# The first Fourier transform of an attention + Fourier mixer kernel: tokens s and 576-s folded before the matmuls

## Chip, cores and metric

One core of a Trainium2 chip. The metric is the time of one execution in microseconds of the device, the median of several runs. Everything is float32 at the interface.

## What is computed

The reference is three layers in a row. The change is in the second, and in the store of the first.

```python
def _moe_ref(x, w_ch1, w_ch2):               # x: (4, 576, 512), the output of the attention
    X = np.fft.fft(x, axis=1)                # over the 576 tokens: "the first transform"
    X = np.fft.fft(X, axis=2)                # over the 512 channels
    mixed = np.real(X).astype(np.float32)
    u = x + mixed
    un = (u - mean(u)) / sqrt(var(u) + 1e-06)
    ch = np.maximum(un @ w_ch1, 0.0) @ w_ch2
    return u + ch
```

Ahead of it stands an attention with 4 batches of 8 heads, 576 tokens and head size 64, and a learned bias; behind it a second mixer (`_moe2_ref`) with a matmul over the tokens.

## The kernel before

The stages follow each other: bias tables, attention, Fourier stage, channel MLP, gated MLP. Float32 products are made of rounded halves ("hi" and "lo", type fp32r), three matmuls for one product.

**Attention.** It walks over 72 pairs of units, one per iteration `d`; `n = d - 72` counts the last ones, and `after(n)` is called at the end of each iteration. Heads are done two at a time, 16 pairs of them (0 to 15), four for each batch. `finish` scales the output of a pair on DVE (L530 to L556), `store` writes it to the DRAM array `xd[b]` (L568, L571) one iteration later. The last pair (15) is not stored: `finish` writes it straight into the Fourier stage's input tile of batch 3 (L556). The last probabilities are transposed on PE (L484), copied by ACT (L486), their low half taken by DVE (L493), and multiplied on PE (L510).

**Loads for the Fourier stage.** `first_folds` calls `Folds.load(0)` at `n` = -3, and `load(1)`, `load(2)`, `load(3)` at `n` = 0, 3 and 4 (`X_LOAD`); each is two transfers on SP's queue (L742, L743), with the 576 tokens on partitions in five blocks `t` of 128. The sine table is loaded at `n` = 0 by POOL (L733), the cosine table during the bias stage (L696).

**Folds.** For real input the second transform needs only sums and differences of channels. `Folds.prep(b)` makes them on DVE in six steps: twice a sum or difference of the upper and lower half (L769, 5 x 256 elements, one operand read backwards), four times a second fold (L757, 635 elements, and L758, 5 elements), ACT rounds it (L759), DVE takes the low part (L763, L764). From `n` = 1 on, two steps for batch 0 are put into each iteration of the attention's end; the other batches' steps stand one by one between the matmul groups of the Fourier stage.

**Fourier stage.** For each batch five groups of the first transform (`p1`, `pe`, `po`, `me`, `mo`; `stage1`, L837), each a sum over the 576 tokens against 290 table columns: four blocks of 128 tokens with three matmuls each, and the last 64 tokens with two, so 14 matmuls. ACT evacuates (L840). `second` is the second transform (L884), `residual` transposes the input on PE (L872), and two DVE additions (L888, L895) write `u`. In batches 2 and 3, weight unpacking (L994 to L1009) and the norm of the first token chunks (L1156 to L1211, with matmuls at L1163) are put into the same places, and then the MLP begins (L1301, L1337).

The order on each engine is set when the program is built, by a list scheduler: an instruction that it takes to be ready can be put ahead of one written earlier. Each engine and each queue then runs in order.

Of the kernel before, what the change touches and what calls it, by code (L numbers as in the profile page):

```python
# [20 lines left out]
DM = 512  # L21
# [323 lines left out]
def attention_phase(tc, nc, io, vs, bias, biasl, raw, xd, ident, last, after, es, right):  # L345
# [172 lines left out]
    def finish(d):  # L518
        c = d % 9
        if c not in (3, 4, 8):  # L520
            return
        ns = (2 * (d // 9), 2 * (d // 9) + 1)
        ns = ns if c == 4 else ns[c // 8 : c // 8 + 1]
        for n in ns:
            if n not in xs:
                xs[n] = xp.tile([128, 5, 128], F32, tag="x", name="x") if n + 1 < len(pairs) else last
        po = outs.pop((d // 9, int(c == 4), int(c == 8)))
        w = 1 if c == 4 else 4
        ri = wp.tile([128, 2, 4], F32, tag="ri", name="ri", bufs=4)[:, :, 0:w]
        nc.vector.tensor_scalar(  # L530
            out=ri, in0=po[:, :, 0:w, 64], scalar1=PSC * 1e-9, scalar2=vs[:, 0:1], op0=ALU.add, op1=ALU.mult
        )
        yield
        nc.vector.reciprocal(out=ri, in_=ri)
        yield
        if c != 4:
            n = ns[0]
            x = xs[n][:, 0:4].rearrange("p t (h d) -> p h t d", h=2)
            nc.vector.tensor_tensor(
                out=x if ahead(n) else x[:, ::-1],  # L540
                in0=po[:, :, :, 0:64],
                in1=ri.rearrange("p h (w o) -> p h w o", o=1).to_broadcast([128, 2, 4, 64]),
                op=ALU.mult,
            )
            return
        for j, n in enumerate(ns):
            x = xs[n]
            if n + 1 < len(pairs):
                nc.vector.tensor_scalar(
                    out=x[:, 4, 0:64], in0=po[:, j, 0, 0:64], scalar1=ri[:, j], scalar2=None, op0=ALU.mult  # L550
                )
                continue
            for a in range(2):
                f = 64 * a if ahead(n) else 64 - 64 * a
                r = slice(64 * a, 64 * a + 64)
                nc.vector.tensor_scalar(  # L556
                    out=x[0:64, 4, f : f + 64], in0=po[r, j, 0, 0:64], scalar1=ri[r, j], scalar2=None, op0=ALU.mult
                )

    def store(d):  # L560
        n = 2 * (d // 9) + (d % 9 == 8)
        if d % 9 not in (4, 8) or n + 1 == len(pairs):
            return
        b, p = pairs[n]
        p = p if ahead(n) else H // 4 - 1 - p
        f = slice(128 * p, 128 * p + 128)
        x = xs.pop(n)
        nc.sync.dma_start(out=xd[b][0:512, f].rearrange("(t p) d -> p t d", p=128), in_=x[:, 0:4])  # L568
        for a in range(2):
            f = 128 * p + (64 * a if ahead(n) else 64 - 64 * a)  # L570
            nc.sync.dma_start(out=xd[b][512:S, f : f + 64], in_=x[64 * a : 64 * a + 64, 4, 0:64])  # L571
# [71 lines left out]
def phases(tc, nc, io, vs, low, raw, xd, ident, tables, last, after, right):  # L643
# [4 lines left out]
    with ExitStack() as es:  # L648
        att = attention_phase(tc, nc, io, vs, bias, biasl, raw, xd, ident, last, after, es, right)
# [26 lines left out]
X_LOAD = 0, 3, 4  # L676
# [5 lines left out]
AFTER = (0,)  # L682


def tables(tc, nc, io, es):
# [4 lines left out]
    tt = cp.tile([128, 10, TP], F32R, name="tt")  # L690

    fs = cp.tile([128, 8, 128], F32, name="fs")
    ident = cp.tile([128, 128], F32, name="ident")

    def load():
        nc.gpsimd.dma_start(out=tt, in_=io["c_t"][:, 0])  # L696
# [4 lines left out]
        nc.sync.dma_start(out=ident, in_=io["c_ident"])  # L701
        yield

    return (tt, fs, ident), load()


class Folds:

    SIZE = 5 * (DM + 1)
    STEPS = 6

    def __init__(self, tc, nc, io, xd, xs, work, temps, es):
        self.tc, self.nc, self.io, self.xd, self.es = tc, nc, io, xd, es
        self.xs = [x.rearrange("p (t f) -> p t f", t=5) for x in xs]
        self.pm = [w.rearrange("p (t f) -> p t f", t=5) for w in work]
        self.temps = [t.rearrange("p (t f) -> p t f", t=5) for t in temps]  # L720
        self.hi, self.lo = [], []
        self.done = -1
        self.flow = self.steps()

    def last(self):

        return self.xs[B - 1][:, :, DM - 127 : DM + 1]

    def open(self):

        p = self.es.enter_context(pool(self.tc, name="ff", bufs=1, side="right"))
        self.sin = p.tile([128, 10, TP], F32R, name="sin")
        self.nc.gpsimd.dma_start(out=self.sin, in_=self.io["c_t"][:, 1])  # L733
        for x in range(2):
            self.hi.append(p.tile([128, 5, DM], F32R, name=f"fhi{x}"))
            self.lo.append(p.tile([128, 4, DM], F32R, name=f"flo{x}"))

    def load(self, b):
        nc, x, d = self.nc, self.xs[b], self.xd[b]
        n = DM if b + 1 < B else DM - 128  # L740
        f = slice(1, n + 1)
        nc.sync.dma_start(out=x[:, 0:4, f], in_=d[0:512, 0:n].rearrange("(k p) d -> p k d", p=128))  # L742
        nc.sync.dma_start(out=x[0:64, 4, f], in_=d[512:S, 0:n])  # L743

    def prep(self, b):
        nc, x, pm = self.nc, self.xs[b], self.pm
        hi, lo = self.hi[b % 2], self.lo[b % 2]
        up, dn = slice(1, 128), slice(255, 128, -1)


        ops = (ALU.add, ALU.subtract, ALU.subtract, ALU.add)
        r = slice(0, 64)

        def high(g):
            s, F = pm[g // 2], self.temps[g % 2]
            c = 128 * (g % 2)
            nc.vector.tensor_tensor(out=F[:, :, 1:128], in0=s[:, :, up], in1=s[:, :, dn], op=ops[g])  # L757
            nc.vector.tensor_copy(out=F[:, :, 0:1], in_=s[:, :, c : c + 1])  # L758
            nc.scalar.activation(out=hi[:, :, 128 * g : 128 * g + 128], in_=F, func=AF.Copy)  # L759

        def low(g):
            F, q = self.temps[g % 2], slice(128 * g, 128 * g + 128)
            nc.vector.tensor_tensor(out=lo[:, :, q], in0=F[:, 0:4], in1=hi[:, 0:4, q].bitcast(F32), op=ALU.subtract)  # L763
            nc.vector.tensor_tensor(  # L764
                out=hi[64:128, 4, q], in0=F[r, 4], in1=hi[r, 4, q].bitcast(F32), op=ALU.subtract
            )

        for z in range(2):
            nc.vector.tensor_tensor(  # L769
                out=pm[z], in0=x[:, :, 256:0:-1], in1=x[:, :, 257 : DM + 1], op=ALU.subtract if z else ALU.add  # L770
            )
            high(2 * z)
            yield
            high(2 * z + 1)
            low(2 * z)
            yield
            low(2 * z + 1)
            yield
# [33 lines left out]
def fft_phase(tc, nc, folds, tabs, ut, bank, extra, es):  # L812
# [7 lines left out]
    tt, fs, ident = tabs  # L820
    xs, need = folds.xs, folds.need
    COS, SIN = tt, folds.sin
# [5 lines left out]
    def stage1(b, nm, col, ncol, t):  # L828
        hi, lo = folds.hi[b % 2], folds.lo[b % 2]
# [12 lines left out]
    def first(b, nm):  # L842
# [3 lines left out]
        need(folds.STEPS * b + dict(p1=2, pe=2, po=2, me=4, mo=5)[nm])  # L846
        stage1(b, nm, *dict(p1=(128, 1, COS), pe=(0, 128, COS), po=(128, 128, SIN), me=(256, 128, COS), mo=(384, 128, SIN))[nm])
# [5 lines left out]
    def gather(b, e):  # L853

        n = 2 * b + e
        if 3 <= n < 2 * B:
            o = 1280 * (n % 2)
            t = parts[n] = room[:, o : o + 1280].rearrange("p (t s c) -> p t s c", t=5, s=2)
# [4 lines left out]
    def residual(b, e, y):  # L863
# [738 lines left out]
def build(tc, io, out):  # L1602
    nc = tc.nc
    with ExitStack() as ctx:
# [14 lines left out]
            [more[:, o : o + 1280], more[:, o + 1280 : o + 2560]],  # L1619
            [raw[:, n : n + 640], more[:, o + 2560 : o + 3200]],  # L1620
            right,
        )
        with ExitStack() as e1:
            e1.enter_context(tc.manual_schedule())
            phases(tc, nc, io, vs, (low, more), raw, xd, tabs[2], load, folds.last(), first_folds(folds), right)
# [76 lines left out]
def consts2():  # L1702
# [7 lines left out]
    tt = np.zeros((128, 2, 10, TP), np.float32)  # L1710
    for n, fn in enumerate((np.cos, np.sin)):
        a = fn(2 * np.pi * ((np.arange(576)[:, None] * t) % 576) / 576)
        h, l = two(a)
        for k in range(4):
            tt[:, n, k] = h[128 * k : 128 * k + 128]
            tt[:, n, 4 + k] = l[128 * k : 128 * k + 128]
        tt[0:64, n, 8] = tt[64:128, n, 8] = h[512:]
        tt[0:64, n, 9] = l[512:]
    c["c_t"] = tt
    d = np.arange(128)[:, None]  # L1720
# [54 lines left out]
```

## Time and profile before

| | us |
|---|---|
| median of 3 runs | 1116.43 (1114.87 to 1120.73) |
| the profiled execution, its own time | 1117.11 |
| its span in the profile | 1115.3 |
| PE busy | 1035.9 (93%) |
| DVE busy | 700.1 (63%) |
| ACT busy | 554.0 (50%) |
| POOL busy | 289.8 (26%) |

The profile's times count from the start of the span. By stage: bias to about 125 us, attention to 382, Fourier stage to about 481, channel MLP to about 900, gated MLP to the end.

### The profile page before, as it was taken

The numbers are of one execution on the slowest core, as the hardware profiler recorded it, in microseconds if no ns is written. First come the engines' busy times: TensorE is split into PE (matmuls) and PEld (weight loads), VectorE is DVE, ScalarE is ACT, GpSimd is POOL, SyncE is SP. The second block draws the span as 40 slices with busy tenths as digits, with TensorE's granted clock in tenths as the row PEclk, the third lists the DMA queues.
The fourth block names the chain that finished last, engine by engine and source line by source line (L and its number), as shares of the span: only waits on it lengthen the run. The fifth ranks groups of instructions, "written<-read, shape, count | busy, mean of one in ns | idle before, by whom it ended". The sixth has DMA issues, their size and how long they took to land.

```text
span 1115.3 us, 25715 instructions
## 1 busy us (share of the span) xinstructions
PE 1035.9 (93%) x10723; PEld 947.7 (85%) x10723; DVE 700.1 (63%) x1821; ACT 554.0 (50%) x1048; POOL 289.8 (26%) x248
## 2 busy tenths in 40 slices
PE   6999888889889799789999999999999999999998
PEld 3778777778788677588999999999999989998997
DVE  5998887888888866567894433324593176262612
ACT  3888797989898335444452111212363144333322
POOL 2777786878684000000000000000002120100000
PEclk8999899999999899879999999999999999999999
DMA  5542087779786600124550000000242000101011
GB/s 164 183 137 92 18 178 161 173 166 186 170 181 152 219 1 1 38 76 133 154 168 1 1 1 1 1 1 1 77 148 59 1 1 1 39 1 48 1 39 48
DMA packets 115490, 89.81 MB, mean 81 GB/s; under 512 B 85545, under 2 KB 95981, under 8 KB 115117
## 3 DMA queue, kind: packets, MB, share of 16 engines
q1 hardware_dynamic: 112360, 79.29, 27.7%
q10 hardware_dynamic: 2724, 5.90, 1.6%
q0 software_dynamic: 288, 2.97, 0.7%
q8 instruction: 84, 1.38, 0.5%
q14 instruction: 34, 0.27, 0.1%
HBM read 58.95 MB, written 9.14 MB: 61 GB/s over the span
## 4 chain that ended last, share of the span: by engine, by line
PE 59%; DVE 5%; ACT 1%; issue 1%; DVEq 0%; ACTq 0%
PE h L1301 18%; PE acc L1337 17%; PE psp L1473 5%; PE pu L1448 4%; PE po L1495 4%; PE y L837 3%; PE pv L1396 3%; PE D L884 2%; PE xs L872 1%; DVE yl L1380 1%; DVE bs L1402 0%; DVE pt L493 0%; DVE wsq L998 0%; DVE ve L944 0%; DVE v L1407 0%
## 5 line engine op out<-in xcount | busy, mean ns | idle before, releaser
L1305 ACT ACTIVATE gh<-h 128x256 fp32r<-128x256 f32 x144 | 55.2, 383 | 245.9 <-PE h L1301 240.2
L1306 DVE SCALAR_TENSOR_TENSOR gl<-h,gh 128x256 fp32r<-128x256 f32 x144 | 60.9, 423 | 175.5 <-ACT gh L1305 175.0
L1301 PE MATMUL h<-uh,wh 128*128 128x256 f32 x576 | 163.2, 284 | 2.2 <-DVE gl L1306 2.0
L1301 PE MATMUL h<-uh,wl 128*128 128x256 f32 x576 | 162.2, 282 | 1.1 <-DVE wl L1009 1.1
L1337 PE MATMUL acc<-gh,wh 128*128 128x256 f32 x576 | 163.0, 283 | 0.0
L1337 PE MATMUL acc<-gh,wl 128*128 128x256 f32 x576 | 161.0, 280 | 1.4 <-DVE wl L1009 1.4
L1301 PE MATMUL h<-ul,wh 128*128 128x256 f32 x576 | 162.1, 282 | 0.0
L1337 PE MATMUL acc<-gl,wh 128*128 128x256 f32 x576 | 160.8, 279 | 0.0
L1093 POOL MEMSET w<- 64x288 f32 x2 | 0.7, 335 | 478.7 <-DVE wsq L1001 478.6
L1301 PEld LDWEIGHTS h<-uh,wh 128*128 128x128 f32 x576 | 110.5, 192 | 3.0 <-DVE gl L1306 2.5
L1301 PEld LDWEIGHTS h<-uh,wl 128*128 128x128 f32 x576 | 109.8, 191 | 1.3 <-DVE wl L1009 1.3
L1301 PEld LDWEIGHTS h<-ul,wh 128*128 128x128 f32 x576 | 110.3, 192 | 0.1
L1337 PEld LDWEIGHTS acc<-gh,wl 128*128 128x128 f32 x576 | 108.4, 188 | 1.7 <-DVE wl L1009 1.7
L1337 PEld LDWEIGHTS acc<-gl,wh 128*128 128x128 f32 x576 | 108.9, 189 | 0.5 <-DVE gl L1306 0.2
L1337 PEld LDWEIGHTS acc<-gh,wh 128*128 128x128 f32 x576 | 108.9, 189 | 0.4
L444 ACT ACTIVATE P<-s,mm 128x576 f32<-128x576 f32 x144 | 103.4, 766 | 3.8 <-DVE mm L436 3.4
L484 PE MATMUL turn<-ident,P 128*128 128x128 f32 x380 | 59.5, 289 | 34.9 <-DVE pt L493 34.5
L461 POOL TENSOR_TENSOR hl<-P,hl 128x1024 f16<-128x1024 f32 x68 | 86.2, 1289 | 20.3 <-ACT hl L455 13.5
L510 PE MATMUL po<-vp,pt 128*128 128x65 f16 (+3 forms) x2324 | 85.0, 196 | 3.1 <-DVE pt L493 0.9
L510 PEld LDWEIGHTS <-pt 128*128 128x128 f16 (+1 forms) x2324 | 81.6, 102 | 6.7 <-issue 2.3
L484 PEld LDWEIGHTS turn<-ident,P 128*128 128x128 f32 x380 | 42.2, 145 | 47.5 <-DVE pt L493 21.5
L250 ACT ACTIVATE mask<-pre 128x576 f16<-128x576 f32 x96 | 61.0, 651 | 25.5 <-PE pre L247 24.3
(245 smaller groups left out, 2672.2 us busy)
## 6 DMA issues: line engine op xcount, KB each, us to landing
w<-in_w_ch SPq DMA_DIRECT2D x32, 512.0 KB, 3.6
vld<-in_v ACTq DMA_DIRECT2D x16, 320.0 KB, 2.9
raw<-in_q SPq DMA_DIRECT2D x16, 320.0 KB, 4.1
raw<-in_v SPq DMA_DIRECT2D x16, 320.0 KB, 3.8
raw<-in_k SPq DMA_DIRECT2D x16, 288.0 KB, 3.3
w<-in_w_in SPq DMA_DIRECT2D x8, 512.0 KB, 3.6
out<-o SPq DMA_DIRECT2D x16, 256.0 KB, 2.0
xd<-x SPq DMA_DIRECT2D x15, 256.0 KB, 3.7
```

The lines of the kernel that those rows point to most:

```text
L250: nc.scalar.activation(out=m.rearrange("p (x e) -> p x e", x=2), in_=p[:, :, 0:288], func=AF.Sigmoid, scale=1e30)
L444: nc.scalar.activation(out=P[:, x, 0:S], in_=s, func=AF.Exp, bias=mm[:, 1, x : x + 1], scale=1.0)
L461: nc.gpsimd.tensor_tensor(out=hl[:, :, o : o + c], in0=P[:, :, j : j + c], in1=hl[:, :, j : j + c], op=ALU.subtract)
L484: nc.tensor.transpose(t[:, 128 * k : 128 * k + 128], P[:, 128 * k : 128 * k + 128], ident)
L510: nc.tensor.matmul(out=po[c, t % 4, 0:w], lhsT=pt[:, x, c], rhs=vp[:, j, hh, f : f + w], start=(i == 0), stop=(i == len(seq) - 1),)
L1301: nc.tensor.matmul(out=h, lhsT=st[:, q], rhs=mv[:, k], start=(n == 0), stop=(n == 11))
L1305: nc.scalar.activation(out=gh, in_=h, func=AF.Relu)
L1306: nc.vector.scalar_tensor_tensor(out=gl, in0=h, scalar=0.0, in1=gh.bitcast(F32), op0=ALU.max, op1=ALU.subtract)
L1337: nc.tensor.matmul(out=acc[x, d // 2][:, d % 2], lhsT=st[:, q], rhs=mv, start=(e == 0 and d % 2 == 0 and n == 0), stop=(e == NF - 1 and d ...
L1448: nc.tensor.matmul(out=p[:, 0:CH], lhsT=st[:, q], rhs=mv[:, kk, e], start=(n == 0), stop=(n == 11))
L1473: nc.tensor.matmul(out=p[:, 0:CH], lhsT=st, rhs=mv, start=(n == 0), stop=(n == len(seq) - 1))
L1495: nc.tensor.matmul(out=p, lhsT=st[:, f, c], rhs=mv, start=(n == 0), stop=(n == 11))
```

## The change

Tokens s and 576-s have the same cosine and opposite sines. So the input is now held as tokens 0 to 288 (three blocks) and, block by block beside them, tokens 576-s (three blocks). DVE adds and subtracts the two, and the first transform then sums over 289 tokens: two blocks of 128 with three matmuls each and one of 33 with two, so 8 matmuls a group; cosine groups take the sum, sine groups the difference.

- The backward rows are fetched by `indirect_dma_start` on POOL: three gathers of 127, 128 and 32 rows of 2 KB for each batch, with a small table of row numbers; POOL also zeroes the rest of the blocks. SP still loads the forward rows.
- The folds have other steps: `total` (1536 elements), `mix` (762, both operands backwards), `fold` (two of 381 and small ones), `low` (514, and 257 on 33 partitions).
- Sine and cosine tables, now half as long, come in one transfer during the bias stage; the one at `n` = 0 is gone.
- The last pair is stored like the others; `load(1)` and `load(2)` are at `n` = 2 and 5, and `load(3)` after the first three groups of the Fourier stage.

```diff
@@ finish, store
-                xs[n] = xp.tile([128, 5, 128], F32, tag="x", name="x") if n + 1 < len(pairs) else last
+                xs[n] = xp.tile([128, 5, 128], F32, tag="x", name="x")
...
-        if d % 9 not in (4, 8) or n + 1 == len(pairs):
+        if d % 9 not in (4, 8):
             return
@@ constants, tables
-X_LOAD = 0, 3, 4
+X_LOAD = 2, 5
+WIDE = 258, 256
-    tt = cp.tile([128, 10, TP], F32R, name="tt")
+    tt = cp.tile([128, 2, 6, TP], F32R, name="tt")
-        nc.gpsimd.dma_start(out=tt, in_=io["c_t"][:, 0])
+        nc.gpsimd.dma_start(out=tt, in_=io["c_t"])
+        nc.sync.dma_start(out=rows, in_=io["c_rows"])
@@ Folds.open
-        self.sin = p.tile([128, 10, TP], F32R, name="sin")
-        self.nc.gpsimd.dma_start(out=self.sin, in_=self.io["c_t"][:, 1])
@@ Folds.load
-        nc.sync.dma_start(out=x[:, 0:4, f], in_=d[0:512, 0:n].rearrange("(k p) d -> p k d", p=128))
-        nc.sync.dma_start(out=x[0:64, 4, f], in_=d[512:S, 0:n])
+        nc.gpsimd.memset(x[:, 2:6:3, f], 0.0)
+        nc.gpsimd.memset(x[0:1, 3, f], 0.0)
+        nc.sync.dma_start(out=x[:, 0:2, f], in_=d[0:256].rearrange("(k p) d -> p k d", p=128))
+        nc.sync.dma_start(out=x[0:33, 2, f], in_=d[256:T2])
+        for k, r in ((3, slice(1, 128)), (4, slice(0, 128)), (5, slice(0, 32))):
+            nc.gpsimd.indirect_dma_start(
+                x[r, k, f], None, d[:, :], bass.IndirectOffsetOnAxis(ap=self.rows[0 : r.stop - r.start, k - 3 : k - 2], axis=0)
+            )
@@ Folds.prep
-        def high(g): ...
-        def low(g): ...
+        def mix(z):
+            nc.vector.tensor_tensor(out=uv, in0=two(254, 129), in1=two(511, -385), op=op)
+        def fold(z):
+            nc.vector.tensor_tensor(out=F[:, :, 1:128], in0=u, in1=v, op=ALU.add)
+            nc.vector.tensor_tensor(out=F[:, :, 129:256], in0=u, in1=v, op=ALU.subtract)
...
+            nc.scalar.activation(out=hi[z][:, :, 0:n], in_=F[:, :, 0:n], func=AF.Copy)
+        def low(z):
+            nc.vector.tensor_tensor(out=l, in0=F[:, 0:2], in1=h[:, 0:2].bitcast(F32), op=ALU.subtract)
+            nc.vector.tensor_tensor(out=h[64:97, 2], in0=F[0:33, 2], in1=h[0:33, 2].bitcast(F32), op=ALU.subtract)
+        def total(z):
+            nc.vector.tensor_tensor(
+                out=self.sums[z], in0=x[:, 0:3, 1 : DM + 1], in1=x[:, 3:6, 1 : DM + 1], op=signs[z]
+            )
+        total(0); yield; mix(0); yield; fold(0); total(1); yield
+        low(0); mix(1); yield; fold(1); yield; low(1); yield
@@ fft_phase
-        for k in range(4):
-            seq += [(hi[:, k, c], t[:, k]), (hi[:, k, c], t[:, 4 + k]), (lo[:, k, c], t[:, k])]
-        seq += [(hi[:, 4, c], t[:, 8]), (hi[:, 4, c], t[:, 9])]
+        for k in range(2):
+            seq += [(hi[:, k, c], t[:, k]), (hi[:, k, c], t[:, 2 + k]), (lo[:, k, c], t[:, k])]
+        seq += [(hi[:, 2, c], t[:, 4]), (hi[:, 2, c], t[:, 5])]
...
     for nm in ("p1", "pe", "po"):
         first(0, nm)
         step()
+    folds.load(B - 1)
```

## Rows read from the trace of the kernel before

**Rows 1.** The page's first part: busy time, share, instructions.
```profile
span 1115.3 us, 25715 instructions
...
PE 1035.9 (93%) x10723; PEld 947.7 (85%) x10723; DVE 700.1 (63%) x1821; ACT 554.0 (50%) x1048; POOL 289.8 (26%) x248
```
**Rows 2.** Windows: busy us of each engine, granted clock, DMA share, GB/s.
```profile
365.00:382.40 17.40, 9.26 (x136) 8.58 (x137) 16.69 (x28) 5.64 (x9) 0.00 (x0) 0.71 0.85 276
382.40:443.30 60.90, 60.90 (x357) 47.07 (x354) 38.85 (x70) 24.32 (x47) 0.00 (x0) 1.00 0.02 8
443.30:450.00 6.70, 4.93 (x34) 4.25 (x34) 5.62 (x10) 3.92 (x7) 0.00 (x0) 1.00 0.00 0
450.00:458.70 8.70, 8.69 (x35) 6.38 (x35) 2.44 (x7) 1.88 (x5) 0.00 (x0) 0.80 0.19 60
```
**Rows 3.** Chain that ended last, Fourier stage: start, us, what.
```profile
382.55 5.60 PE y L837 x42
...
439.38 1.94 PE y L837 x14
...
443.31 0.67 ACT d L886
...
451.67 3.51 PE y L837 x14
```
**Rows 4.** Timeline of PE: start, us, what, idle before.
```profile
370.79 1.33 PE L484 MATMUL turn<-ident,P 128*128 128x128 f32 x5 [4.54 <-DVE pt L493]
...
450.01 0.67 PE L1163 MATMUL y<-w,ones 128*128 128x256 f32 x2 [1.77 <-DVE w L1159]
```
**Rows 5.** Groups by line, 382 to 470 us: busy us, mean ns, idle.
```profile
L769 DVE TENSOR_TENSOR lowb<-lowb 128x1280 f32<-128x1280 f32 x5 | 7.4, 1485 | 0.0
...
L757 DVE TENSOR_TENSOR raw<-lowb 128x635 f32<-128x635 f32 x6 | 4.9, 820 | 0.2
...
L763 DVE TENSOR_TENSOR flo<-lowb,fhi 128x512 fp32r<-128x512 f32 x6 | 4.2, 693 | 1.0 <-ACT fhi L759 0.9
...
L764 DVE TENSOR_TENSOR fhi<-raw,fhi 64x128 fp32r<-64x128 f32 x6 | 1.7, 285 | 0.1
```
**Rows 6.** Timeline of DVE, end of the attention.
```profile
364.91 0.57 DVE L556 TENSOR_SCALAR lowb<-po,ri 64x64 f32<-64x64 f32 x2
365.51 1.49 DVE L769 TENSOR_TENSOR lowb<-raw 128x1280 f32<-128x1280 f32 x1
...
369.91 1.56 DVE L493 TENSOR_TENSOR pt<-turn,pt 128x640 f16<-128x640 f32 x2
...
373.78 1.49 DVE L769 TENSOR_TENSOR lowb<-lowb 128x1280 f32<-128x1280 f32 x1
...
383.98 0.69 DVE L539 TENSOR_TENSOR lowb<-po,ri 128x512 f32<-128x512 f32 x1
```
**Rows 7.** Timelines of DVE, then of POOL, bias stage.
```profile
74.00 0.75 DVE L235 TENSOR_TENSOR mask<-win,bn 128x576 f16<-128x576 f32 x1
...
78.70 1.88 DVE L235 TENSOR_TENSOR mask<-win,bn 128x576 f16<-128x576 f32 x1
...
78.55 1.41 POOL L238 TENSOR_TENSOR z<-win,bn 128x576 bf16<-128x576 f32 x1
```
**Rows 8.** Groups by line of POOL; last, its timeline.
```profile
L733 POOL DMA_DIRECT2D sin<-in_c_t x1 | 0.6, 609 | 7.2 <-ACT P L444 7.2
...
L1422 POOL MEMSET one<- 128x512 f32 x1 | 0.5, 531 | 0.0
...
L1763 POOL MEMSET const-float32-0.0<- 128x1 f32 x1 | 0.1, 104 | 0.2 <-issue 0.2
...
349.72 2.52 POOL L461 TENSOR_TENSOR hl<-P,hl 128x1024 f16<-128x1024 f32 x2 [3.12 <-ACT hl L455]
```
**Rows 9.** DMA issues: count, KB each, us from issue to landing.
```profile
lowb<-xd SPq DMA_DIRECT2D x2, 1024.0 KB, 9.3
...
xd<-x SPq DMA_DIRECT2D x30, 16.0 KB, 5.5
```

More of the change, by code (lines that the diff above doesn't have):

```diff
@@ L342, in bias_phase, with attention_phase @@
             evict(blk - 1)
-def attention_phase(tc, nc, io, vs, bias, biasl, raw, xd, ident, last, after, es, right):
+def attention_phase(tc, nc, io, vs, bias, biasl, raw, xd, ident, after, es, right):
     vp = es.enter_context(pool(tc, name="vp", bufs=1))
@@ L547, in finish @@
             x = xs[n]
[L548 to L558, printed above, removed]
+            nc.vector.tensor_scalar(
+                out=x[:, 4, 0:64], in0=po[:, j, 0, 0:64], scalar1=ri[:, j], scalar2=None, op0=ALU.mult
+            )
     def store(d):
         n = 2 * (d // 9) + (d % 9 == 8)
-        if d % 9 not in (4, 8) or n + 1 == len(pairs):
+        if d % 9 not in (4, 8):
             return
@@ L640, in attention_phase, with phases @@
         after(d - nd)
-def phases(tc, nc, io, vs, low, raw, xd, ident, tables, last, after, right):
+def phases(tc, nc, io, vs, low, raw, xd, ident, tables, after, right):
     n = 2 * H * S
@@ L648, in phases @@
     with ExitStack() as es:
-        att = attention_phase(tc, nc, io, vs, bias, biasl, raw, xd, ident, last, after, es, right)
+        att = attention_phase(tc, nc, io, vs, bias, biasl, raw, xd, ident, after, es, right)
         ready = False
@@ L701, in load, with __init__ @@
         nc.sync.dma_start(out=ident, in_=io["c_ident"])
+        nc.sync.dma_start(out=rows, in_=io["c_rows"])
         yield
-    return (tt, fs, ident), load()
+    return (tt, fs, ident, rows), load()
 class Folds:
-    SIZE = 5 * (DM + 1)
+    SIZE = 6 * (DM + 1)
     STEPS = 6
-    def __init__(self, tc, nc, io, xd, xs, work, temps, es):
+    def __init__(self, tc, nc, io, xd, xs, work, rows, es):
         self.tc, self.nc, self.io, self.xd, self.es = tc, nc, io, xd, es
[L718 to L721, printed above, removed]
+        self.xs = [x.rearrange("p (t f) -> p t f", t=6) for x in xs]
+        self.sums = [work.rearrange("p (t f) -> p t f", t=3)]
+        self.hi, self.lo, self.rows = [], [], rows
@@ L722, in __init__ @@
         self.done = -1
         self.flow = self.steps()
-    def last(self):
-        return self.xs[B - 1][:, :, DM - 127 : DM + 1]
     def open(self):
         p = self.es.enter_context(pool(self.tc, name="ff", bufs=1, side="right"))
-        self.sin = p.tile([128, 10, TP], F32R, name="sin")
-        self.nc.gpsimd.dma_start(out=self.sin, in_=self.io["c_t"][:, 1])
+        self.sums.append(p.tile([128, 3, DM], F32, name="dif"))
+        self.uv = [p.tile([128, 3, 2, 127], F32, name=f"uv{z}") for z in range(2)]
@@ L745, in prep @@
     def prep(self, b):
-        nc, x, pm = self.nc, self.xs[b], self.pm
+        nc, x = self.nc, self.xs[b]
         hi, lo = self.hi[b % 2], self.lo[b % 2]
[L748 to L759, printed above, removed]
@@ L761, in low, with two @@
-        def low(g):
-            F, q = self.temps[g % 2], slice(128 * g, 128 * g + 128)
-            nc.vector.tensor_tensor(out=lo[:, :, q], in0=F[:, 0:4], in1=hi[:, 0:4, q].bitcast(F32), op=ALU.subtract)
+        signs = ALU.add, ALU.subtract
+        def mix(z):
+            w, uv, op = self.sums[z], self.uv[z], signs[z]
+            def two(start, step):
+                return bass.AP(
+                    tensor=w.tensor, offset=w.offset + start, ap=[list(w.ap[0]), [DM, 3], [step, 2], [-1, 127]]
+                )
+            nc.vector.tensor_tensor(out=uv, in0=two(254, 129), in1=two(511, -385), op=op)
@@ L766, in low @@
             )
[L768 to L778, printed above, removed]
+        total(0)
+        yield
+        mix(0)
+        yield
+        fold(0)
+        total(1)
+        yield
+        low(0)
@@ L780, in steps @@
+        mix(1)
+        yield
+        fold(1)
+        yield
+        low(1)
+        yield
     def steps(self):
@@ L819, in fft_phase @@
     ps_x = es.enter_context(pool(tc, name="ps_x", bufs=2, space=PSUM))
-    tt, fs, ident = tabs
+    tt, fs, ident, _ = tabs
     xs, need = folds.xs, folds.need
-    COS, SIN = tt, folds.sin
+    COS, SIN = tt[:, 0], tt[:, 1]
     ys, Ds = {}, {}
@@ L845, in first @@
             nc.scalar.activation(out=x[:, :, 0:1], in_=x[:, :, 256:257], func=AF.Copy)
[L846 to L847 removed]
+        need(folds.STEPS * b + (5 if nm in ("po", "mo") else 3))
+        stage1(b, nm, *dict(p1=(256, 1, 0), pe=(0, 128, 0), po=(0, 128, 1), me=(128, 128, 0), mo=(128, 128, 1))[nm])
     room = xs[0].rearrange("p t f -> p (t f)")
@@ L1624, in build @@
             e1.enter_context(tc.manual_schedule())
-            phases(tc, nc, io, vs, (low, more), raw, xd, tabs[2], load, folds.last(), first_folds(folds), right)
+            phases(tc, nc, io, vs, (low, more), raw, xd, tabs[2], load, first_folds(folds), right)
         tail(tc, nc, io, folds, tabs, low, right, out, ctx)
```

52 lines of the change are left out of this document (33 added, 19 removed).

## The prediction

> **What bounds the kernel now.** I read the page's first part, then windows by stage, then the chain that ended last, then the timelines of PE and DVE around the change. PE is the busy engine, 93% of the span [rows 1], but an average over stages says little, so the windows come first. From 382.4 to 443.3 us, which is the Fourier stage for batches 0 to 2, PE is busy for all of 60.90 us at full clock (1.00), DVE for 38.85 and ACT for 24.32 [rows 2]. The chain in this stretch is nothing but matmuls in the order written, from the 42 of the first three groups (5.60 us) to the 14 of batch 3's `p1` at 439.38 [rows 3]. So a matmul taken out here is worth its own time, as long as DVE, now 64% busy, keeps up.
>
> On both sides it is otherwise. Just before, from 365.0 to 382.4, DVE is busy for 16.69 of 17.40 us and PE for 9.26, at a mean clock of 0.71 [rows 2]: the folds of batch 0 share DVE with the attention's last subtractions. A fold starts at 365.51, the next subtraction L493 comes at 369.91 [rows 6], and PE's transposes wait for it, idle 4.54 us before 370.79 [rows 4]. After 443.3 the chain goes over to ACT and DVE (ACT's copy at 443.31 [rows 3]); DVE is busy for 5.62 of 6.70 us and PE for 4.93 [rows 2], and PE waits 1.77 us for DVE at 450.01 [rows 4].
>
> **The matmuls taken out.** 42 matmuls take 5.60 us [rows 3], so one costs 0.133 us. A group goes from 14 to 8: 6 x 0.133 = 0.80 us. Sixteen groups lie in the stretch that PE bounds (five each of batches 0 to 2, and batch 3's `p1`): 16 x 0.80 = **-12.8**. Of batch 3's other four groups, `pe` and `po` run under the DVE work of 443.3 to 450.0, and `mo` under the same kind of work later: nothing, and what covers them is DVE's 5.62 us. `me`, at 451.67, is on the chain and runs at half clock: 14 in 3.51 us [rows 3], 0.251 each, in a window with a mean granted clock of 0.80 [rows 2]. Six fewer are 1.5 us. But the clock rose only after `me`, so if that moment stays, the shorter `me` leaves some of the slow time to the matmuls behind it. Bounds 0.7 and 1.5; I take **-1.1**.
>
> **The folds on DVE.** 1280 elements take 1485 ns and 635 take 820 [rows 5]: 1.03 ns an element and 0.165 us fixed; L769 reads one operand backwards at that rate, so backward reads cost nothing extra (both operands backwards is not shown; twice the rate for the two `mix` would be +1.6 us of DVE a batch, in its slack). Before, a batch costs 2 x 1.485 + 4 x (0.82 + 0.165 + 0.693 + 0.285) = 10.8 us. After: twice `total` 1.75, `mix` 0.95, two folds 1.11, one and a half small ones 0.25, `low` 0.69 + 0.43, so 2 x 5.18 = 10.4 us. DVE's work per batch hardly changes. What changes is its density: 38.85 - 3 x 0.4 = 37.6 us of work in some 48 us instead of 60.9, 78%.
>
> At the attention's end the same sums give 0.4 us less, and the last pair's two writes at 364.91 (0.57 together [rows 6]) become one, 0.28 less. The first two steps are also shorter (1.75 + 0.95 against 4.4 us until 369.91 [rows 6]), which lets L493 and PE's transposes go earlier, but the later steps are longer. I take **-0.7**, bounds 0 and -3.5 (if the earlier L493 is kept to the end).
>
> **The gathers.** No gather is in the trace. From below, a plain DMA issue on POOL: 0.61 us [rows 8]. From above, a row of the gather costs as much as the shortest POOL instruction, 104 ns [rows 8]: 287 rows are 29.8 us a batch. A gather is one instruction whose rows are work of one kind, as the 1024 elements of L461 are, so I stay near the issue: about 1 us each. The memsets, from 512 elements in 0.53 us [rows 8], are 1.6 us a batch. POOL is free from 349.72 + 2.52 = 352.2 on [rows 8]. Batch 0's rows are then asked for by about 357, eight us before the first fold at 365.5, and batches 1 and 2 follow at once: nothing on the path. If `total` had to wait for them, what stands behind it on DVE is L493, and behind that PE's last transposes.
>
> DVE and POOL get in each other's way: an L235 on DVE takes 0.75 us alone and 1.88 us when it starts 0.15 us behind POOL's L238 of 1.41 us; it ends 0.62 us after POOL's [rows 7]. So a fold can wait for a whole POOL instruction. POOL's three instructions for one batch may fall into the attention's end: between 0 and 3 x 0.61 = 1.8 us; I take **+0.5**. The Trainium skill ("SBUF — State Buffer", "SBUF: two separate sides") says that the port pair shared by the two is held for the whole instruction by whichever starts first. By that rule, too, the loss is at most the POOL instructions' own length; the trace agrees (0.75 against 1.88).
>
> **The loads moved.** `load(1)` now stands on SP's queue behind pair 14's store, whose data leaves DVE at about 365, so it is issued near 366 instead of 358. It moves half of what took 9.3 us [rows 9], and lands between 371 and 375. Before, batch 1's first fold was pulled forward to 373.78 [rows 6]; if it is again, DVE may wait for it: 0 to 2.5, I take **+0.5**. Work covers the rest: `load(2)` has over 20 us. The last pair's store follows its scaling at 383.98 [rows 6], lands about 5.5 us later [rows 9], and `load(3)` then has until about 410 (ten of sixteen groups, 382 + 10/16 x 48 = 412), so some 20 us. SP's weight loads stand behind it and are needed later still. The sine table's transfer, gone from the most crowded window (DMA share 0.85 [rows 2]), gives something back there, which I count as nothing because DVE bounds that window.
>
> **Hand-offs at the faster pace.** Groups of 1.07 us leave less room for ACT's evacuation and DVE's additions, which free PSUM. From 0 to the second rival's price below; I take **+0.5**.
>
> **Sum.** -12.8 - 1.1 - 0.7 + 0.5 + 0.5 + 0.5 = -13.1, against the profiled execution's 1117.1: 1104.0. The median is 0.7 below that execution, so the forecast for a median is **1103.3 us**. Nothing behind 481 depends on absolute time, so the gain is carried to the end.
>
> **Rivals.**
>
> *The gathers bound the stage (slower).* At 104 ns a row the four batches need 4 x (29.8 + 1.6) = 126 us of POOL, and batch 3's rows arrive at 478 instead of being there at 410: 68 us, 1171. It decides from the point where batch 3 is 13 us late: (423 - 352.2)/4 = 17.7 us a batch, less the memsets 16.1, that is 56 ns a row. Against it: POOL's 1024-element subtraction takes 1.26 us [rows 8], about 1.2 ns an element, so work inside one instruction is far cheaper than instructions. Chance 0.07.
>
> *Batch 0's rows come late.* If a gather of 127 rows of 2 KB (260 KB) is moved by one of the 16 DMA engines, then at 276/0.85/16 = 20.3 GB/s each [rows 2] it takes 12.8 us; asked for at 354.4, it lands at 367.2, about 2 us after DVE wants it. 1105.5, and up to 1109 with slower issues. The Trainium skill ("DMA: Bandwidth & Descriptors", "Why a DMA increments its semaphore by 16 and not by 1") says that 127 partitions put a whole transfer on one engine, with some software-generated copies excepted; by it the sum would be the 1105.5 of this rival. No row shows which holds for a gather. Chance 0.13.
>
> *DVE and ACT become the limit.* At 78% in strict order, an addition that frees PSUM can stand behind a `total` and a fold, 2.9 us. Half of that on average, twice a batch, three batches: 8.6 us given back, 1108 to 1112. For it: the chain already goes over to DVE at 443.3. Against it: two input tiles and two group tiles in PSUM give some 4 us of room. Chance 0.10.
>
> *Nothing moves.* The list scheduler pulls other work (weights, norms) into the gap and the stage ends where it did: 1113 to 1117. Against it: the chain holds no such work before 443. Chance 0.04.
>
> The forecast case, 1098.5 to 1106, has 0.66. The low end is -12.8 - 1.5 - 3.5 with no cost added. The range, 1098.5 to 1109.5, takes in the late rows and half of the third rival, and leaves out 0.16. A difference of 0.5% (5.6 us) is about what can be told from none here. Faster by over that, below 1110.8: 0.66 + 0.13 + 0.06 = 0.85; same: 0.08; slower: 0.07.
>
> **What will show it.** Matmuls at the group line: 160 instead of 280, still about 0.133 us each; PE busy without gaps in a stretch of about 48 us; three POOL gathers a batch of about 1 us; first `total` at about 365 with no wait for a DMA; DVE's busy share there near 78%. The forecast is wrong if DVE stands before the first `total`, if PE's chain in the stage shows DVE or ACT links, or if the windows behind it grow.

## The result, and the profile after

The changed kernel takes 1130.6 us (median; 1126.16 to 1131.97) against 1116.28 for the kernel before, run beside it: 1.0127 of it, 95% interval 1.0103 to 1.0151. It is 1.3% slower, where a gain of 13 us was forecast. The profiled execution took 1126.16 us, its span is 1124.4, 9.1 more than before [rows 1]. The medians are 14.3 us apart, so the stretches below account for 9.1 of these.

The page's first part, after: PE has less to do and POOL more, as forecast, and the span is longer all the same.
```profile
span 1124.4 us, 25515 instructions
...
PE 1027.7 (91%) x10603; PEld 938.3 (83%) x10603; DVE 697.5 (62%) x1808; ACT 549.2 (49%) x1040; POOL 313.6 (28%) x267
```
Windows of the end of the attention, of the Fourier stage up to batch 3's `p1`, and from there to the MLP's first `h` (columns as in [rows 2]):
```profile
366.70:395.95 29.25, 9.93 (x138) 9.17 (x136) 16.60 (x25) 4.39 (x7) 10.97 (x9) 0.64 0.26 71
395.95:446.40 50.45, 46.08 (x243) 34.00 (x241) 34.72 (x58) 20.52 (x38) 7.07 (x5) 0.97 0.20 62
446.40:486.70 40.30, 28.13 (x108) 19.45 (x107) 23.33 (x50) 17.05 (x34) 0.00 (x0) 0.72 0.09 27
```
In the middle window PE stands still for 4.4 us, where before it was busy in every one of 60.90 us [rows 2]; in the last it runs at a mean clock of 0.72.

I cut both executions at the same four instructions: the last 15 `po` matmuls L510 ahead of the first fold, the first `y` matmul, the first of batch 3's `p1`, and the MLP's first `h`. In us:

| stretch | before | after | measured | forecast |
|---|---|---|---|---|
| to the last 15 `po` | 365.62 | 367.32 | +1.7 | 0 |
| from there to the first `y` | 16.77 | 28.63 | +11.9 | +0.3 |
| batches 0, 1, 2 | 17.0, 20.1, 19.8 | 14.5, 18.0, 17.9 | -6.5 | -11.5 |
| batch 3's `p1` to the first `h` | 37.84 | 40.27 | +2.4 | -1.9 |
| first `h` to the end | 638.15 | 637.73 | -0.4 | 0 |

The forecast column sorts the terms of the prediction's sum (start: folds, port, load; batches: 15 groups of 0.80 and the hand-offs; behind: `p1` and `me`). So three stretches went wrong: the start by 11.6 us, the batches by 5.0, what stands behind them by 4.3.

**The start.** DVE's timeline (start, us, what, idle before and what ended it):
```profile
366.70 0.48 DVE L548 TENSOR_SCALAR x<-po,ri 128x64 f32<-128x64 f32 x2
375.61 1.76 DVE L772 TENSOR_TENSOR lowb<-raw 128x1536 f32<-128x1536 f32 x1 [8.43 <-DMA raw<-xd,rows]
...
378.27 1.55 DVE L493 TENSOR_TENSOR pt<-turn,pt 128x640 f16<-128x640 f32 x2
...
391.15 1.76 DVE L772 TENSOR_TENSOR lowb<-lowb 128x1536 f32<-128x1536 f32 x1 [4.09 <-DMA lowb<-xd,rows]
393.99 1.56 DVE L493 TENSOR_TENSOR pt<-turn,pt 128x640 f16<-128x640 f32 x2
```
The first `total` waits 8.43 us for the gathered rows of batch 0, and batch 1's `total`, pulled ahead, another 4.09. Behind each, in DVE's order, stands a subtraction L493 of the attention, and PE waits for that: the first time with its transposes L484, the second with its matmuls L510. PE's timeline:
```profile
379.15 1.33 PE L484 MATMUL turn<-ident,P 128*128 128x128 f32 x5 [11.20 <-DVE pt L493]
...
394.87 1.27 PE L510 MATMUL po<-vp,pt 128*128 128x65 f16 x20 [5.54 <-DVE pt L493]
395.95 0.68 PE L848 MATMUL y<-tt,fhi 128*1 128x290 f32 x2
```
In the kernel before the first of these waits was 4.54 us [rows 4] and the second 0.88:
```profile
381.49 1.06 PE L510 MATMUL po<-vp,pt 128*128 128x65 f16 x20 [0.88 <-DVE pt L493]
```
So the two waits grew by 11.3 us, nearly all that the start lost. Two `y` matmuls take 0.68 us here, at half clock; in the kernel before they took 0.43. (The five transposes took 1.33 us there as well [rows 4].) Why the rows are late, three views show: POOL's timeline; the DMA view (median us from issue to landing last); and the DMA view of single windows, 383 to 385 us first, then 401 to 406 (packets, MB, share of 16 engines; q0 carries the gathers, q1 SP's transfers):
```profile
355.59 2.66 POOL L734 DMA_INDIRECT raw<-xd,rows  x1 [0.20 <-POOL raw L729]
358.56 0.97 POOL L734 DMA_INDIRECT raw<-xd,rows  x1 [0.31 <-issue]
359.83 0.88 POOL L734 DMA_INDIRECT raw<-xd,rows  x1 [0.30 <-issue]
...
374.91 2.57 POOL L734 DMA_INDIRECT lowb<-xd,rows  x1 [12.81 <-issue]
```
```profile
lowb<-xd,rows POOLq DMA_INDIRECT x9, 13.7
raw<-xd,rows POOLq DMA_INDIRECT x3, 16.5
```
```profile
q0 software_dynamic: 12, 0.05, 6.2%
...
q0 software_dynamic: 30, 0.12, 5.8%
q1 hardware_dynamic: 25, 0.01, 0.8%
```
The gathers are asked for in time, from 355.59 on. Those of 128 and 32 rows cost POOL about 1 us, as forecast; the 127-row one costs 2.6. But they land 13.7 to 16.5 us later. From 383 to 385 us batch 1's gather is alone in flight. It takes 6.2% of the 16 engines, which is one engine, and moves 25 GB/s; at that rate the 260 KB of 127 rows take 10.4 us. The next batch's gathers wait 12.81 us on POOL, with nothing shown that they wait for; they go out when the first ones have landed.

**The last pair's store** is slowed too, 8.39 us in the chain, against a median of 4.3 us for the 256 KB stores of this execution. While it is in flight (401 to 406 us, the last two lines above), the two queues together keep about one engine of 16 busy: the store's rest stands beside batch 2's gather. ACT's first `d` waits for it; that tile probably lies where the pair's `x` was (no view shows addresses). The batches hardly lose by it: PE idles for 0.12 us in batch 0, and batch 1 takes 18.0 us, against 17.9 in e1, where the wait is gone.
```profile
399.13 8.39 DMA xd<-x
```
```profile
407.60 0.66 ACT L897 ACTIVATE d<-D 128x580 f32<-128x580 f32 x1 [4.07 <-DMA xd<-x]
```

**The batches.** The chain of waits, batch 1 to the start of batch 2 (start, us, what):
```profile
415.22 0.87 DVE uv L751
416.11 0.56 DVE F L756
...
424.40 0.42 DVE fhi L769
424.82 0.03 issue
424.85 0.77 DVE lowa L899
...
426.20 1.70 ACT raw L872 x2
427.90 0.04 issue
427.94 0.61 PE xs L883 x3
428.56 1.15 PE y L848 x8
```
Before, this chain was matmuls alone [rows 3]. Now DVE's fold steps hold it for some 10 us (with one rounding on ACT among them), then comes the addition L899, then ACT's copies of token tiles, L872, and only then PE's transposes.

### The profile page after: what moved, and what is told of

The parts are those of the page before. It is cut to its first block, busy times and chain, and to the rows that moved or that the text cites. A ratio compares the mean times of both kernels' runs of the same rounds, so it can differ in the third digit from the quotient of the medians.

```text
span 1124.4 us, 25515 instructions
## 1 busy us (share of the span) xinstructions
PE 1027.7 (91%) x10603; PEld 938.3 (83%) x10603; DVE 697.5 (62%) x1808; ACT 549.2 (49%) x1040; POOL 313.6 (28%) x267
## 2 busy tenths in 40 slices
DMA packets 119616, 89.23 MB, mean 79 GB/s; under 512 B 89860, under 2 KB 100232, under 8 KB 119372
## 4 chain that ended last, share of the span: by engine, by line
PE 64%; DVE 16%; POOL 7%; issue 5%; ACT 4%; DMA 4%; ACTq 0%; SPq 0%; POOLq 0%; DVEq 0%
PE h L1313 18%; PE acc L1349 17%; PE psp L1485 5%; PE pu L1460 4%; PE po L1507 4%; PE pv L1408 3%; POOL hl L461 3%; PE sc L408 3%; PE po L510 2%; PE turn L484 2%; DVE bt L311 2%; DVE mask L235 2%; PE bps L267 1%; PE D L895 1%; DMA win<-in_c_win 1%
## 5 line engine op out<-in xcount | busy, mean ns | idle before, releaser
L484 PE MATMUL turn<-ident,P 128*128 128x128 f32 x380 | 60.1, 291 | 41.6 <-DVE pt L493 41.2
L510 PE MATMUL po<-vp,pt 128*128 128x65 f16 (+3 forms) x2324 | 86.3, 198 | 7.2 <-DVE pt L493 5.5
L510 PEld LDWEIGHTS <-pt 128*128 128x128 f16 (+1 forms) x2324 | 83.1, 103 | 10.6 <-DVE pt L493 5.7
L484 PEld LDWEIGHTS turn<-ident,P 128*128 128x128 f32 x380 | 42.6, 146 | 54.4 <-DVE pt L493 29.3
L486 ACT ACTIVATE pt<-turn 128x640 f16<-128x640 f32 x76 | 53.1, 698 | 43.1 <-PE turn L484 42.7
```

Source lines behind the costliest of these rows:

```text
L484: nc.tensor.transpose(t[:, 128 * k : 128 * k + 128], P[:, 128 * k : 128 * k + 128], ident)
L486: nc.scalar.activation(out=pts[u][:, 0:5], in_=t, func=AF.Copy)
L510: nc.tensor.matmul(out=po[c, t % 4, 0:w], lhsT=pt[:, x, c], rhs=vp[:, j, hh, f : f + w], start=(i == 0), stop=(i == len(seq) - 1),)
```

## The experiments

Theory A: the 127 rows go through one DMA engine, and the rows are late for that alone. Theory B: gathers are slow as such. Theory C: DVE and ACT bound the faster stage. "Start" below is from the last 15 `po` to the first `y`; "batches" are from one batch's `p1` to the next; "behind" is from batch 3's `p1` to the first `h`. These stretches are compared, not spans: the attention, which no edit touches, ends anywhere from 365.6 to 375.4 us in these executions. Ratios are to the kernel before on the same chip.

**e1, 128 rows.** Token 0 comes in as its own partner.
```diff
-        nc.gpsimd.memset(x[0:1, 3, f], 0.0)
-        for k, r in ((3, slice(1, 128)), (4, slice(0, 128)), ...
+        for k, r in ((3, slice(0, 128)), (4, slice(0, 128)), ...
@@ tables: row 0 of the cosine table * 0.5; row numbers 0, 575, 574, ...
```


> The changed kernel, but the 127-row gather fetches 128 rows (token 0 comes in as its own partner, and row 0 of the cosine table is halved, so the output is unchanged). Theory A (the 127 rows all go through one of 16 DMA engines): the stretches with a DMA share of 0.06 at 23 to 29 GB/s vanish, the first total no longer waits 8.43 us nor the second 4.09, the first y matmul goes from 395.95 back to 382 to 386, and the time is 1106 to 1114 us. Theory B (software gathers are slow as such: issue, one behind another): the waits of 8.4 and 4.1 us stay within 2 us, and so does the time, 1124 to 1131. Theory C (DVE and ACT bound the faster stage): the start comes back as in A, but the stage from the first y matmul to its end still lasts about 90 us, time 1114 to 1120.

0.994 (0.9912 to 0.9967), median 1111.42. Start 15.76, 1.0 better than before; batches 13.0, 17.9, 17.9; behind 40.4. The DMA view and POOL's timeline:
```profile
lowb<-xd,rows POOLq DMA_INDIRECT x9, 4.7
raw<-xd,rows POOLq DMA_INDIRECT x3, 5.6
```
```profile
353.88 1.07 POOL L733 DMA_INDIRECT raw<-xd,rows  x1 [0.28 <-POOL raw L728]
...
358.61 0.96 POOL L733 DMA_INDIRECT lowb<-xd,rows  x1 [0.27 <-POOL lowb L728]
```
One row more, and the gathers land in about 5 us, the next batch's go out at once, and DVE's waits for rows are gone. The software queue's packets change as well; in the DMA view of the whole execution (packets, MB, share) it has, changed kernel first, then e1:
```profile
q0 software_dynamic: 4752, 4.16, 1.3%
...
q0 software_dynamic: 912, 4.14, 1.1%
```
The page counts 89860 packets under 512 B in the changed kernel and 86020 in e1, so all 3840 more are small. They pass at the start of a gather (378 to 379 us: DMA share 0.29 at 8 GB/s), so the 10 us at one engine's share aren't theirs. A holds, B falls. But C holds as well: batches 1 and 2 miss the forecast's 16.1 and 15.8 by 2 us each. PE's timeline shows the places:
```profile
411.64 0.61 PE L882 MATMUL xs<-ident,raw 128*128 128x128 f32 x3 [1.61 <-ACT raw L871]
...
429.58 0.62 PE L882 MATMUL xs<-ident,raw 128*128 128x128 f32 x3 [2.17 <-DVE lowa L905]
```

**e8, the 127 rows in two gathers** of 112 and 15, all else as in the change.
```diff
-        for k, r in ((3, slice(1, 128)), (4, ...
+        for k, r in ((3, slice(1, 113)), (4, ...), (5, ...), (6, slice(113, 128))):   # 6: block 3, a fourth column of row numbers
```


> The changed kernel with its 127-row gather cut into two, of 112 and 15 rows; tables, memsets and arithmetic stay as in the change. Theory A (127 rows go through one DMA engine; nothing else made the 128-row run better): gathers land in about 5 us and not 13.7, the first y matmul comes 15.5 to 17 us after the last 15 matmuls before the wait (28.6 in the changed kernel, 15.8 with 128 rows), and the time is that of the 128-row run within 4 us, 1107 to 1115. If that run gained by the memset or row 0 it left out, this one stays with the changed kernel, 1124 to 1131.

Start 15.78, gathers land in 5.3 to 5.5 us: the number of rows in one gather is the cause, not the memset or row 0, nor that it starts at partition 1 (the 112 rows do too). An earlier form of this edit, e4, gave no time. The time is 0.9977 (0.9954 to 1.0000), 1116.94, above what A expected; in the profiled execution (1123.61) the batches are 13.0, 18.3, 20.6, behind 41.2. Batch 2 had PE 10.00 of 10 us busy from 420 to 430 at a clock of 0.81.

**e2, plain loads in place of the gathers** (forward rows, so the sums are over other tokens).
```diff
+        nc.sync.dma_start(out=x[:, 3:5, f], in_=d[320:S].rearrange("(k p) d -> p k d", p=128))
+        nc.sync.dma_start(out=x[0:32, 5, f], in_=d[288:320])
```


> The changed kernel with plain loads on SP's queue (two transfers of 128-row blocks and 32 rows) in place of the gathers; it fetches the rows in forward order, so the folds work on other tokens than the reference wants. All other work is the same. This is the bound for a gather that costs nothing on POOL. If the gathers are all that went wrong (A or B), the time is 1104 to 1112; against the 128-row run A expects at most 4 us less, B 12 us or more less. If it stays above 1114, then the hand-offs of DVE and ACT (C) or the later stores of the last pairs hold the stage, and not the gathers.

0.9977 (0.9943 to 1.0011), 1116.48. Start 15.73, the same as with 128-row gathers: a gather of 128 rows costs this stage nothing. Batches 13.0, 18.3, 20.7, behind 41.2, so the rest lies with C and with the clock (PE is busy for all of 415 to 420 us at 0.50).

**e3, the kernel before with 8 matmuls a group** (token blocks 2 and 3 are left out of the sums).
```diff
-        for k in range(4):
+        for k in range(2):
             seq += [(hi[:, k, c], t[:, k]), (hi[:, k, c], t[:, 4 + k]), (lo[:, k, c], t[:, k])]
```


> The kernel before with 8 matmuls a group in place of 14 (it leaves out token blocks 2 and 3 from the sums), loads and folds as before. This measures the matmul term alone: if 6 matmuls in 16 groups are worth 0.80 us each and one more 1.1, 1101 to 1104 us. If DVE and ACT bound the faster stage (C), the stage gives back part: 1106 to 1112. If other work fills the gap, 1114 to 1116.

1.0038 (1.0008 to 1.0069): the cut alone gains nothing. Batch 0 goes from 17.0 to 13.0, the whole 4.0 us of five groups, but batches 1 and 2 become 22.8 and 20.2 and the stretch behind 39.2. PE waits 3.19 us for ACT's `y` copy in batch 1, and the clock is 0.76 and 0.73 from 410 to 430. All that the matmuls gave in batch 0 comes back as waits and as a lower clock.

**e5, 14 matmuls a group in the 128-row kernel** (the first six are done twice, so the output is another one; the expectation counted 16, but the list grows by its first six entries, so it is 14, as before the change).
```diff
-        seq += [(hi[:, 2, c], t[:, 4]), (hi[:, 2, c], t[:, 5])]
+        seq += [(hi[:, 2, c], t[:, 4]), (hi[:, 2, c], t[:, 5])] + seq
```


> The kernel with 128-row gathers, with each group's 8 matmuls done again up to 16 in one accumulation (so it doubles the sums: the output is not the reference's). All else the same; it puts back 8 matmuls of 0.133 us, 1.07 us a group. If matmuls are worth their full time in this stage, each batch gets 5.3 us longer, and the time 17 to 18 us, 1126 to 1130. If PE already waits for DVE and ACT (C), the first batch gets 5.3 us longer (18.3), the next two only 1 to 3.5 us (19 to 21.5), and the tail behind batch 3's p1 2 to 4 us shorter since the granted clock stays at 1.00 for longer: 1112 to 1120.

1.0000 (0.9975 to 1.0025). Batches 17.0, 20.2, 19.7: those of the kernel before to 0.1 us, PE busy for 56.61 of 56.92 us. So new folds, gathers and loads cost nothing as long as PE has 14 matmuls a group. Behind batch 3's `p1` this kernel takes 36.4 us, 4.0 less than with 8. PE's timelines, first of e5, then of e1, show how:
```profile
449.12 0.67 PE L1174 MATMUL y<-w,ones 128*128 128x256 f32 x2 [1.82 <-DVE w L1170]
452.63 3.67 PE L894 MATMUL D<-y,fs 128*128 128x290 f32 x12
```
```profile
442.44 1.19 PE L1174 MATMUL y<-w,ones 128*128 128x256 f32 x2 [3.45 <-DVE w L1170]
447.20 4.31 PE L894 MATMUL D<-y,fs 128*128 128x290 f32 x12
```
With 8 a group PE waits longer for DVE's norm sums, and the norm's matmuls run at half clock, 1.19 against 0.67; the mean granted clock of the stretch is 0.72 against 0.87.

**e6, no copies of token tiles on ACT** (PE transposes the tile itself).
```diff
-        if 3 <= n < 2 * B:
+        if 3 <= n < 0:
```


> The kernel with 128-row gathers, without ACT's copies L871 of the token tiles of batches 1.5 to 3 (PE transposes the tile itself, with stride 2; the output is unchanged). PE waits 1.6 and 2.2 us for these copies or for DVE's mirror behind them in batches 1 and 2. If ACT's queue (d, then the copies) is the hold, the batches go from 17.9 to 16.2 to 16.8 us and the time falls by 2 to 5 us. If DVE's string of fold steps is the hold, PE waits for L905 or L898 instead, the batches stay at 17.5 to 18 and the time within 2 us.

0.9895 (0.9858 to 0.9931), 1108.69. Batches 13.7, 16.5, 16.4, with no wait of PE over 0.3 us in them: ACT's queue was the hold, and the forecast's 16.1 and 15.8 are almost there.

**e7, e9, e10: fewer steps of the MLP's weight and norm work between the groups**, on top of e6.
```diff
-X_STEPS = 4
+X_STEPS = 2        # e9: 1, e10: 3
```


> The run before with 2 in place of 4 steps of the MLP's weight and norm work put between the groups once the folds are done. Behind batch 3's p1 PE waits 3.45 and 2.11 us for DVE's norm sums, which stand behind weight conversions on DVE. If these conversions are in the way, the waits fall below 2 and 1.3 us as in the kernel before, and the stage ends 2 to 3 us earlier; if the norm chain itself is the bound, or the weights are then late for the MLP, no gain or up to 4 us more.

> 128-row gathers, no copies L871, and 1 in place of 4 steps of weight and norm work between the groups. With 2 the stretch from batch 3's p1 to the first h took 34.0 us, with 4 39.2. If DVE's and ACT's weight conversions between the groups are what makes PE wait and its clock fall, 1 gives 33 to 35 us and the time 1100 to 1104. If the norm sums, which are among these steps, set the end, they come later: 36 to 42 us, 1104 to 1112.

> The same with 3 steps. If the stretch depends on how much work stands in DVE's queue, it lies between the 34.0 us of 2 steps and the 39.2 of 4: 35 to 38 us, 1103 to 1107. If it depends on whether the granted clock falls at a certain wait or not, it is near one of the two.

Behind batch 3's `p1`: 39.2 us with 4 steps (e6), 33.0 with 3, 34.0 with 2, 30.8 with 1. Times: 0.9890 (0.9838 to 0.9941), 0.9867 (0.9832 to 0.9903) and 0.9841 (0.9783 to 0.9899) for 3, 2 and 1. These intervals overlap each other and e6's, so the times alone don't rank them. The stretch comes from one execution each, but the four kernels with 1 step (e9, e12, e13, e16) all have 30.8 to 31.4. The work was in the way, and with 1 step it is not missed later (636.6 us behind the first `h`, 638.15 in the kernel before). But 3 comes out ahead of 2, so the stretch isn't simply proportional to what stands in DVE's queue.

**e11, the same two edits on the kernel before** (no copies, 2 steps).

> The kernel before, with only the two later edits: no copies L871 and 2 steps of extra work in place of 4. If these are worth something only once the matmuls are cut (PE bounds the batches in the kernel before), the batches stay at 57 us, and at most the tail of 37.8 us gets 1 to 3 us shorter: 1113 to 1118. If they are worth as much here, 1106 to 1110, and little of what the best version gained belongs to the folding.

1.0003 (0.9980 to 1.0025). Batches 17.0, 20.4, 20.3, behind 34.3: in the profiled execution the shorter stretch is eaten by batches 0.8 us longer and by 643.5 us behind the first `h` against 638.15. Why it is slower there isn't settled; the runs here that keep 4 steps take 636.2 to 641.1. Without the fold the two edits bring nothing that the medians show.

**e12, e13: the e9 kernel again, and with the 127-row gather.**

> The fastest version so far again, in more rounds: 128-row gathers, no copies L871, 1 step of extra work. 0.980 to 0.988 of the kernel before; over 0.99 the first result was luck.

> The same version with the change's 127-row gather in place of the 128-row one. Theory A: the rows come late as in the changed kernel, the first y matmul 11 to 14 us later, batch 0 at half clock at first (14.5 in place of 13), so 11 to 16 us more than the version beside it: 1111 to 1116, ratio 0.993 to 1.0. If the one-engine gather mattered only because the stage behind it was short of DVE and ACT, at most 6 us more.

0.9928 (0.9907 to 0.9949) and 0.9967 (0.9949 to 0.9986), on another chip than e9's: over the 0.99 that was to mark e9's 0.984 as luck. Start 15.75 against 28.32, the batches and the stretch behind equal to 0.6 us, as A expects; yet the medians are only 5.4 us apart, which is the other alternative's number (at most 6) and not A's 11 to 16. In the profiled executions the rest went in the attention, which ended 6.3 us later in e12 than in e13: PE stands still nine times for 0.2 to 0.5 us between 358 and 369 with nothing shown that it waits for, and its clock is half from 364 on:
```profile
358.98 0.55 PE L510 MATMUL po<-vp,pt 128*128 128x64 f16 x13 [0.46 <-issue]
...
363.59 0.62 PE L510 MATMUL po<-vp,pt 128*128 128x65 f16 x12 [0.53 <-issue]
```

**e14, e15, e16: the changed kernel, e1 and e9 side by side on one chip.**

> The changed kernel itself, beside the two versions below on one chip. If its loss is a property of the kernel, 1.008 to 1.016 of the kernel before.

> The changed kernel with 128-row gathers. By the traces the stretch from attention's last matmuls to the first h is 14 to 15 us shorter than in the changed kernel (11.9 to 12.9 at the start, 1.6 in the batches): if nothing in the attention pays for it, 13 to 16 us less than the run above, 0.994 to 1.002. If timely gathers cost the attention something (as between the two versions that differ in nothing else, 5.4 us in the medians against 12 in the stage), 5 to 8 us less.

> The same without the copies L871 and with 1 step of extra work. By the traces 10 us less than the run above in the stage (48.8 to 46 or 47.4 in the batches, 40.4 to 30.8 behind them): 8 to 12 us less, 0.984 to 0.993. If PE's idle instants behind 358 us and its half clock there come with this version and not with a chip, the trace shows them again.

| kernel | median | ratio | start | batches | behind |
|---|---|---|---|---|---|
| before | 1117.67 | 1 | 16.77 | 17.0, 20.1, 19.8 | 37.84 |
| changed (e14) | 1127.95 | 1.0098 | 28.49 | 14.9, 18.3, 18.7 | 37.3 |
| 128 rows (e15) | 1116.44 | 0.9976 | 15.95 | 15.1, 18.3, 18.9 | 40.3 |
| e9's edits too (e16) | 1099.31 | 0.9839 | 15.75 | 13.0, 16.4, 16.4 | 31.2 |

(The stretches of before are those of its own profiled execution; the other three profiled executions took 1123.55, 1119.71 and 1098.77.) The late gather costs 11.5 us of median and 12.5 of start, as A says; the edits to ACT's and DVE's queues bring 17.1 more. Not all of the 17.1 is shown to be theirs: e15's first batch began at a mean clock of 0.53 (384.97 to 390.00), and took 15.1 us, where the same code in e1 ran it at 1.00 in 13.0. And the 128-row kernel alone, 0.994 on e1's chip, is 0.9976 here, as e2 and e8 were, so what e8 lies above A's range is no more than one code's scatter between chips. The last row beats both kernels: 0.984 came back here, if not on e12's chip, and PE's gaps of e12 don't appear. The windows of e16's stage:
```profile
382.60:428.40 45.80, 45.53 (x243) 34.67 (x240) 34.88 (x58) 15.91 (x32) 3.34 (x3) 1.00 0.17 56
428.40:459.60 31.20, 22.42 (x108) 16.52 (x107) 22.61 (x50) 13.77 (x30) 0.00 (x0) 0.87 0.12 35
```
PE is busy for 45.53 of 45.80 us at full clock, the picture that the forecast drew (no gaps in about 48 us), with DVE at 76% (it said 78).

## Why the prediction was wrong

**The gathers: this step failed.** It priced what a gather costs POOL, about 1 us, and for 128 and 32 rows that is right (six of the eight took 0.87 to 0.97 us); the 127-row ones took 2.6, so batch 0's last issue ended at 360.71 and not by 357. It then took the rows as there because they had been asked for eight us ahead. They land 13.7 to 16.5 us after the issue. The rival "batch 0's rows come late" had the mechanism and too small a price: 2 us and a chance of 0.13, where the start lost 11.9. Its 12.8 us for the transfer were too many for an engine alone (10.4 at 25 GB/s), but the engine isn't alone: it shares the bursts of other transfers, and from the issue at 355.59 to the first `total` 20 us pass. And the rival counted DVE's wait once. It came twice (8.43 and 4.09), each time ahead of L493, with PE idle behind it for 11.20 and 5.54 us, where it had been 4.54 and 0.88. The prediction had named this queue ("what stands behind it on DVE is L493"), but didn't cost it. e1, e8 and e13 against e12 show the cause: with 128 or 112 and 15 rows the start is 15.8, with 127 it is 28.3 to 28.6.

The rule cited there from the Trainium skill ("DMA: Bandwidth & Descriptors", "Why a DMA increments its semaphore by 16 and not by 1") takes the largest k up to 16 that divides the outermost size on both sides of the transfer, here the number of rows. The runs agree: one engine for 127 rows, and fast landings for 128 and for 112 and 15 (16 and 15 engines by the rule, which no row here counts).

**The matmuls taken out.** 0.80 us a group is right: batch 0 goes from 17.0 to 13.0 in e1 and e3, and with the copies gone batches 1 and 2 gain 3.7 and 3.4 (e6). In the changed kernel batch 0 took 14.5, as it began at half clock (0.51 from 395.95 to 399). That PE's long wait brought the half clock isn't shown: with rows in time the first batch takes anything from 13.0 (e1, e16, clock 1.00) to 14.5 and 15.1 (e12, e15, clock 0.88 and 0.84). Batches 1 and 2 took 2 us each more than forecast.

**Hand-offs at the faster pace.** This step failed by its size: +0.5 in the sum, 4.0 measured in batches 1 and 2, where the third rival's mechanism, DVE and ACT as the limit, was given 0.10 (its price is the one that the term calls the second rival's). It isn't DVE's total, 76% in e16, but the order: ACT's copies of token tiles (L871 in e1) stand behind a copy of `d` that waits for DVE's L898, and that one behind 10 us of fold steps (e6 took the copies out and the wait went). The rival priced this at 8.6 us over three batches; half came.

**Batch 3's `me`, and what is behind it.** Forecast -1.9, measured +2.4; this step failed too. It took `me` as free-standing. But the batches end sooner, DVE's weight conversions then stand in front of the norm sums (PE waits 3.44 us against 1.77 [rows 4]), and more of the stretch runs at the lower clock, a mean of 0.72 over it against 0.84 before. With fewer conversions between the groups it is 30.8 to 34.0 (e7, e9, e10). How much of it is the order and how much the clock isn't separated: no run changed one without the other.

**The folds and the port.** -0.7 and up to +1.0 of costs were forecast; the start with timely rows is 1.0 shorter. The steps take what was worked out: `total` 1.76 us, and `mix` 0.95, so both operands backwards cost nothing. No loss by the port shows. **The loads moved:** batch 1's wait for its rows came, but from the gather (4.09), and the last pair's store took 8.39 us, which made ACT wait 4.07 for the `d` tile. Not foreseen; gone in e1.

**The forecast as a whole** fits another kernel: e16, with 128-row gathers and two more edits, is 18.4 us faster than the kernel before, more than the 13.1 of the sum.

**Open:** what makes the clock fall in the batches in some executions (e2, e8, e15) and not in e1, which has e15's code and a wait of 1.6 us; PE's gaps in e12, and why the same code made 0.984 on two chips and 0.993 on a third.

## What to carry to other kernels

Count the rows of a transfer before its bytes: gathers with one of 127 rows among them landed after 13.7 us, with one of 128 after 4.7, and the long one held stores and the next gathers too; pad or split it. Work taken out of the bounding engine is worth its time only until the next queue in strict order comes up, so cost what stands in front of each instruction on the other engines at the new pace, and move that too. And follow a late transfer through the queue it blocks: here DVE's 12.5 us of waiting held up attention work that PE needed.

## What the runs showed that was not expected

- An indirect gather of 127 rows of 2 KB runs at 25 GB/s on one DMA engine and holds POOL for 2.6 us; one of 128 rows holds it about 1 us, and lands in about 5. The 127-row gathers also bring 3840 more packets under 512 B.
- Gathers queued behind it went out only when it had drained (12.81 us), and a store beside one took 8.39 us where 4.3 is usual.
- Six matmuls more in every group made the stretch behind batch 3's `p1` 4.0 us shorter (e5 against e1); PE waited less there, and its mean clock was 0.87 against 0.72.
